# Quarter-array attention scores gathered into one burst per batch, with their exponentials in a ring of their own

## The chip, the cores and the metric

The kernel runs on one core of one Trainium2 chip. The metric is the device time of one execution in microseconds (us); the value used is the median over several runs. A profile of one execution gives the busy times and the chain of waits; its span is 2.1 us shorter than the measured time of the same execution (581.1 against 582.92 us in the run that was profiled, 583.22 us in the median).

## What is computed

```python
def _attn_ref(q, k, v, tau):                     # 8 batches, 12 heads, 448 rows, head size 64
    q_n = q / (np.linalg.norm(q, axis=-1, keepdims=True) + 1e-06)
    k_n = k / (np.linalg.norm(k, axis=-1, keepdims=True) + 1e-06)
    scores = np.matmul(q_n, k_n.transpose(0, 1, 3, 2)) / tau
    attn = np.exp(scores - np.max(scores, axis=-1, keepdims=True))
    attn = attn / (np.sum(attn, axis=-1, keepdims=True) + 1e-09)
    return np.matmul(attn, v)

def _moe_ref(x, U, V, w_ch1, w_ch2):             # x: 8 x 448 x 768, the heads side by side
    h = x.transpose(0, 2, 1) @ U @ V             # low-rank mixing of the rows
    u = x + h.transpose(0, 2, 1)
    return u + np.maximum(u @ w_ch1, 0.0) @ w_ch2    # 768 -> 3072 -> 768
```

The change touches the scores, their exponentials and the product with v, in batches 2 to 7.

## The kernel before, in words

Every operation is first recorded as an `Op` with an engine, an assumed duration, the operations that it depends on, and the ring slots that it acquires and releases. `Plan.run` (L156) then simulates the engines with these assumed durations and fixes the order of the instructions on each engine; the hardware executes each engine's queue in that order. On TensorE there are several streams, each in its own order, and the planner takes the first stream whose head is ready: products with v (`pe_av`) stand ahead of scores (`pe_sc`), and scores ahead of the mixer (`pe_mlp`), so that attention of a later batch is woven into the mixer of an earlier one. `PE`'s order is thus a single line of matmuls, in which the mixer fills all the room.

The stages of a batch b:

- Loads and normalisation: q and k are loaded on the POOL queue (`load_qk`, L493), scaled on VectorE into `xn` (L618), and from batch 2 on transposed by a DMA from the SP queue (L633) into `qkT`. The ring `r_qkT` (L334) has six buffers, one per head pair of a batch; a buffer comes free when the score bursts that read it are issued.
- Scores (`scores`, L661): the 448 keys of a head are cut into three chunks of 128 and a rest of 64. A slot `(p, c)` with c of 0 to 2 is a row slot: two matmuls of 64 rows by 128 columns of the array, one per head of pair p, side by side in the upper and the lower half of the array. A slot `(p, 3)` with p even is a quarter slot: four matmuls of 64 rows by 64 columns, the rest keys of the four heads of pairs p and p+1, one in each quarter of the array (`parts`, L656). All matmuls stream 448 columns. Each slot fills two PSUM banks (`r_sc`, L381, banks 0 to 5), so a burst of three slots takes six banks and is one `Op` on TensorE, planned at 0.2 us and 0.189 us per slot (L680). `groups_of` (L1052) cuts the 21 slots of a batch into seven bursts of three. `mlp` (L994 to L999) ties the bursts to positions in the second product of the mixer two batches earlier (`SPOTS`).
- Exponentials: one ScalarE activation per slot (L695), from PSUM into `attn`. The ring `r_attn` (L326, L329) has three tiles of four chunks; the rest chunk of an even pair also serves the odd pair, so the tile of an even pair is held until the odd pair's products are done (uses 4 against 2, L671).
- Values (`values`, L700): per head 16 matmuls (4 row tiles by 4 key chunks, L718) into one PSUM bank of `r_av2` (L383), then a reciprocal and a multiplication on VectorE (L746, L748) into `X`.
- Mixing (`stage0`, L789): a projection (L801), a product (L851), additions into `u` (L865), a DMA transpose into `uT` (L886). The first burst of a batch also waits for the last products of L851 of the batch before (`first_v`, L1070).
- The mixer (`mlp`, L907): the first product with w_ch1 (L928), a ReLU on ScalarE or VectorE (L951, L953), the second product with w_ch2 (L964), additions (L975), stores (L989).

The bursts of a batch before the change, with pairs written as p.c, are 0.0 0.1 0.2 | 1.0 1.1 1.2 | 0.3 2.0 2.1 | 2.2 3.0 3.1 | 3.2 2.3 4.0 | 4.1 4.2 5.0 | 5.1 5.2 4.3.

Of the kernel before, what the change touches and what calls it, by code (L numbers as in the profile page):

```python
# [269 lines left out]
def kernel(  # L270
# [14 lines left out]
    B, H, S, D = q.shape  # L285
# [3 lines left out]
    NPAIR = H // 2  # L289
# [3 lines left out]
    SC = 4  # L293
    SCH = S // SC
# [5 lines left out]
    BURST = [1] + [2] + [3] * 6  # L300
    SPOTS = {8: [(6,)] * 7 + [()], 6: [(5, 17), (10,), (6,), (6,), (6,), (6,)]}
    WIDE = 2
    RAW_KEYS = {(0, 0), (0, 1)}
    FILL = 0.7

# [6 lines left out]
    def fixed(n, shape, dt, name):  # L312

        tiles = [const.tile(shape, dt, name=f"{name}{i}") for i in range(n)]
        return tiles
# [5 lines left out]
    def fixed_ring(tiles):  # L321
        return Ring(len(tiles), lambda i: tiles[i % len(tiles)])

    ld_t = fixed(3, [SCH, 2, G, SC * D], BF, "qk_nat")
    xn_t = fixed(3, [SCH, 2 * SC, 128], BF, "xn")
    attn_t = fixed(3, [128, SC, 2, 512], BF, "attn")  # L326
    v_t = fixed(2, [128, H, SC, D + 8], BF, "v_nat")

    r_ld, r_xn, r_attn = fixed_ring(ld_t), fixed_ring(xn_t), fixed_ring(attn_t)  # L329
    r_sq = ring(2, [SCH, G // 2, SC * D], BF, "sq")  # L330
    r_ss = ring(4, [SCH, 2, G, SC], FP, "ss")
    r_ln = ring(4, [SCH, 2, G, SC], FP, "ln")
# [29 lines left out]
    r_rd = ring(2, [128, 4, 1], FP, "rd")  # L362
# [3 lines left out]
    def bank_ring(groups, cap, shape=None):  # L366
        def make(g):
            if len(g) > 1:
                return bank_t[:, g[0]:g[-1] + 1, :]
            t_ = bank_t[:, g[0], :]  # L370
            if shape is not None:
                t_ = t_[:, 0:shape[0] * shape[1]].rearrange("p (a b) -> p a b", a=shape[0])
            return t_
        return BankRing(banks, groups, cap, make)

    r_mm = bank_ring([(7,), (6,), (5,), (4,)], 3)
    r_av = bank_ring([(5,), (6,), (7,), (4,)], 2, (4, D + 8))
    r_av0 = bank_ring([(5,), (6,)], 2, (4, D + 8))
    r_av5 = bank_ring([(5,), (6,), (0,), (1,), (2,), (3,)], 2, (4, D + 8))
    r_z = bank_ring([(7,), (4,), (6,), (5,), (3,), (1,), (2,), (0,)], 4)  # L380
    r_sc = bank_ring([(0, 1), (2, 3), (4, 5)], 3)  # L381
    r_low = bank_ring([(5,), (4,), (3,), (2,), (1,), (0,)], 2)
    r_av2 = bank_ring([(5,), (4,), (3,), (2,), (1,), (0,), (6,)], 2, (4, D + 8))  # L383
    r_up = bank_ring([(7,), (6,), (5,), (4,), (3,), (2,), (1,), (0,)], 4)
    r_out = bank_ring([(7,), (6,), (5,), (4,)], 4)
# [23 lines left out]
    plan = Plan()  # L409
# [14 lines left out]
    def pe_t(n):  # L424
        return n / 2400.0 + 0.0025
# [222 lines left out]
        return list(ops.values())  # L648


    attns, bursts = {}, {}

    def members(b, slots):
        return sorted({p for p, _ in slots} | {p + 1 for p, c in slots if b >= WIDE and c == SC - 1})
# [6 lines left out]
    def scores(b, slots, then=()):  # L661

        off = PAD * (b % 2)
        scs = [Slot(r_sc, 2 if (b, p) in RAW_KEYS else 1) for p, _ in slots]
        sets = {p: got[b, p, "qkT"] for p in members(b, slots)}
        ready = []
        for x in sets.values():
            ready += x[1]
        ready += then
        for p in sets:  # L670
            attns.setdefault((b, p), (Slot(r_attn, 2 if b < WIDE or p % 2 else 4), []))  # L671

        def score():
            for (p, c), sc in zip(slots, scs):
                for hh, q_, n0, w, out in parts(b, p, c, sc):
                    qkT, r = sets[q_][0], slice(D * hh, D * hh + D)
                    nc.tensor.matmul(out=out, lhsT=qkT.tile.rearrange("p b s -> p (b s)")[r, n0:n0 + w],  # L677
                                     rhs=qkT.tile[r, SC:2 * SC, :].rearrange("p c s -> p (c s)"),
                                     start=True, stop=True)
        o = plan.add(Op("PE", 0.2 + pe_t(S) * len(slots), score, deps=ready, acq=scs + [attns[b, p][0] for p in sets],  # L680
                        rel=[x[0] for x in sets.values()]), pe_first if b == 0 else pe_sc)
        o.big = len(slots) > 2
        if o.big:
            bursts.setdefault(b, []).append(o)
        for (p, c), sc in zip(slots, scs):
            _, _, (inv, a, scaled) = sets[p]
            attn, exps = attns[b, p]
            if (b, p) in RAW_KEYS:
                for hh in range(2):
                    exps.append(plan.add(Op("ACT", act_t(S, 0.143), lambda sc=sc, c=c, hh=hh, attn=attn, inv=inv, a=a: nc.scalar.activation(  # L690
                        out=attn.tile[0:SCH, c, hh, off:off + S], in_=sc.tile[0:SCH, hh, 0:S], func=AF.Exp,
                        scale=inv.tile[:, 1, a + hh, c:c + 1]), deps=[o, scaled], acq=[attn],
                        rel=[sc, inv], prio=0.1)))
                continue
            exps.append(plan.add(Op("ACT", act_t(2 * S, 0.08), lambda sc=sc, c=c, attn=attn: nc.scalar.activation(  # L695
                out=attn.tile[0:SCH if b < WIDE else 128, c, :, off:off + S],
                in_=sc.tile[0:SCH if b < WIDE else 128, :, 0:S], func=AF.Exp),
                deps=[o], acq=[attn], rel=[sc], prio=0.1 if b == 0 else 1)))

    def values(b, p, X):  # L700
        off = PAD * (b % 2)
        attn, exps = attns[b, p]
        even, kp = attn, SCH
        if b >= WIDE:
            kp = 128
            if p % 2:
                even = attns[b, p - 1][0]
                exps = exps + attns[b, p - 1][1]
        last_exp[b] = exps[-1]
        if b == 0 and p == 0:  # L710
            last_exp["first"] = [exps[0]]
        muls = []
        heads = []
        for hh in range(2):
            heads.append((Slot(r_av2 if BURST[b] > 2 else r_av if b else r_av5 if p == NPAIR - 1 else r_av0, 1), Slot(r_rd, 1)))

        def product(h, hh, t, j, av, start):
            nc.tensor.matmul(out=av.tile[:, t, 0:D + 1],  # L718
                             lhsT=(attn if j < SC - 1 else even).tile[0:kp, j, hh, 128 * t:128 * (t + 1)],
                             rhs=v_t[b % 2][0:kp, h, j, 0:D + 1], start=start, stop=(j == SC - 1),  # L720
                             skip_group_check=ends)
        ends = b == 0 and p == NPAIR - 1
        ready = attn_set + v_set[b]
        if ends:
            for j in range(SC):
                for hh, (av, rd) in enumerate(list(heads)):
                    h = 2 * p + hh

                    def fn(h=h, hh=hh, j=j, av=av):
                        for t in range(4):  # L730
                            product(h, hh, t, j, av, j == 0 and t == 0)
                    o = plan.add(Op("PE", 4 * 0.033, fn, deps=[exps[j]] + got[b, h, "v"] + ready,
                                    acq=[av] if j == 0 else [], rel=[attn] if j == SC - 1 else []), pe_av)
                    if j == SC - 1:
                        heads[hh] += (o,)
        for hh in range(2):
            h = 2 * p + hh
            av, rd = heads[hh][:2]
            o = heads[hh][-1]
            for t in () if ends else range(4):  # L740
                for j in range(SC):
                    first, last = t == 0 and j == 0, t == 3 and j == SC - 1
                    o = plan.add(Op("PE", 0.033, lambda t=t, j=j, h=h, hh=hh, av=av: product(h, hh, t, j, av, j == 0),
                        deps=exps + got[b, h, "v"] + ready if first else (), acq=[av] if first else [],
                        rel=([attn] if even is attn else [attn, even]) if last else []), pe_av)
            r = plan.add(Op("DVE", 0.20, lambda av=av, rd=rd: nc.vector.reciprocal(  # L746
                out=rd.tile, in_=av.tile[:, :, D:D + 1]), deps=[o], acq=[rd], prio=1))
            muls.append(plan.add(Op("DVE", dve_t(256), lambda av=av, rd=rd, h=h: nc.vector.tensor_mul(  # L748
                X.tile[:, :, h * D:(h + 1) * D], av.tile[:, :, 0:D],
                rd.tile.to_broadcast([128, 4, D])), deps=[r],  # L750
                acq=[X], rel=[av, rd], prio=1)))
        last_av[b, p] = o
        return muls
# [298 lines left out]
    def groups_of(b):  # L1052
        if b < WIDE:
            slots = [(p, c) for p in range(NPAIR) for c in range(SC)]
            return [slots[n:n + BURST[b]] for n in range(0, len(slots), BURST[b])]
        slots = []
        for p in range(0, NPAIR, 2):
            slots += [(p, 0), (p, 1), (p, 2), (p + 1, 0), (p + 1, 1), (p + 1, 2), (p, 3)]
        return [slots[n:n + BURST[b]] for n in range(0, len(slots), BURST[b])]

    def go(b, h0, h1, vs=True):
        return stats(b, h0, h1, *load_qk(b, h0, h1), hold=after if b == 1 else ())
# [123 lines left out]
```

## Time and profile before

| | |
|---|---|
| time, median of 3 runs (lowest, highest) | 583.22 us (582.8, 583.4) |
| span of the profiled execution | 581.1 us |
| instructions of TensorE, matmuls | 4871 |
| DVE (VectorE) busy | 292.5 us, 50% |
| ACT (ScalarE) busy | 284.9 us, 49% |
| exponentials L695, 128 x 896 | 166, mean 916 ns |
| granted TensorE clock | full over the whole span |

Durations of single matmuls in the profile overlap[...]. What a matmul costs is read from the start of one to the start of the next, and so from the starts in the timeline; "busy" counts the union of the rows. The timeline merges neighbouring instructions of one line into one row with their number.

### The profile page before, as it was taken

Reading aid. Unit: us, or ns where it says so; the run is one execution under the profiler, and the core shown is the slowest. Engines: PE = TensorE matmul, PEld = TensorE weight load, DVE = VectorE, ACT = ScalarE, POOL = GpSimd, SP = SyncE. Lnnn points to the kernel's source line nnn. Section 1 sums busy time; section 2 is a strip of 40 time slices with the busy share of each in tenths; the row PEclk is TensorE's granted clock in tenths of the full one; section 3 lists DMA queues with packets and bytes.
Section 4 is the critical chain, followed back from the end, with each engine's and each line's share of the span. In section 5 each row is a group of like instructions: output and inputs, shape, how many; then the busy total and the mean of one; then the engine's idle time right before and its main releaser. Section 6 shows DMA issues by size and latency. Waiting matters only on the chain.

```text
span 581.1 us, 11713 instructions
## 1 busy us (share of the span) xinstructions
PE 572.8 (99%) x4871; PEld 327.3 (56%) x4871; DVE 292.5 (50%) x690; ACT 284.9 (49%) x471; POOL 92.9 (16%) x134
## 2 busy tenths in 40 slices
PE   8899999999999999999999999999999999999997
PEld 6565556445655665554466655655456666654565
DVE  8989829999756676557434760343102240100011
ACT  7967754777625671466543645434454334024300
POOL 7334240161050132003300140000000000000000
PEclk9999999999999999999999999999999999999999
DMA  9999992999594469346945573231040100310021
GB/s 156 200 207 191 210 162 69 147 119 116 91 128 107 65 80 145 73 78 79 81 99 91 105 49 68 61 74 33 0 69 28 42 15 11 86 41 1 1 54 56
DMA packets 133429, 50.69 MB, mean 87 GB/s; under 512 B 98304, under 2 KB 133376, under 8 KB 133376
## 3 DMA queue, kind: packets, MB, share of 16 engines
q0 software_dynamic: 72256, 25.73, 39.0%
q1 hardware_dynamic: 61056, 24.19, 20.3%
q8 instruction: 38, 0.62, 0.5%
q14 instruction: 15, 0.12, 0.1%
q10 hardware_dynamic: 64, 0.02, 0.0%
HBM read 52.25 MB, written 11.01 MB: 109 GB/s over the span
## 4 chain that ended last, share of the span: by engine, by line
PE 94%; DMA 2%; DVE 2%; POOL 1%; issue 0%; ACT 0%; DVEq 0%; POOLq 0%
PE bank L964 38%; PE bank L928 37%; PE bank L718 8%; PE bank L677 7%; DMA v_nat<-in_v_dram 2%; PE bank L851 2%; PE bank L474 1%; POOL qk_nat L496 1%; PE bank L801 1%; POOL v_nat L516 0%; DVE xn L618 0%; DVE qkT L1005 0%; PE bank L772 0%; DVE ss L550 0%; DVE X_sb L748 0%
## 5 line engine op out<-in xcount | busy, mean ns | idle before, releaser
L964 PE MATMUL bank<-w_sb,relu 128*128 128x384 bf16 (+1 forms) x1368 | 231.6, 323 | 0.3 <-DVE X_sb L748 0.2
L928 PE MATMUL bank<-uT,w_sb 128*128 128x512 bf16 (+1 forms) x1152 | 231.8, 353 | 0.0
L695 ACT ACTIVATE attn<-bank 128x896 bf16<-128x896 f32 (+1 forms) x166 | 141.0, 916 | 97.8 <-PE bank L677 97.6
L964 PEld LDWEIGHTS <-relu 128*128 128x128 bf16 x1368 | 128.6, 98 | 90.2 <-issue 12.5
L928 PEld LDWEIGHTS <-w_sb 128*128 128x128 bf16 x1152 | 109.1, 98 | 102.3 <-issue 7.6
L951 ACT ACTIVATE relu<-bank 128x384 bf16<-128x384 f32 (+1 forms) x156 | 84.6, 543 | 129.6 <-PE bank L928 129.2
L975 DVE TENSOR_TENSOR O_sb<-bank,u_nat 128x384 f32<-128x384 f32 (+1 forms) x57 | 31.2, 549 | 183.3 <-PE bank L964 165.1
L550 DVE TENSOR_REDUCE ss<-sq 112x8 f32<-112x512 bf16 x96 | 62.5, 674 | 1.6 <-ACT sq L544 1.2
L618 DVE TENSOR_TENSOR xn<-qk_nat,inv 112x512 bf16<-112x512 bf16 x93 | 60.6, 681 | 0.6 <-DMA qkT<-xn 0.5
L718 PEld LDWEIGHTS <-attn 128*128 128x128 bf16 (+1 forms) x1536 | 54.2, 97 | 10.7 <-issue 3.4
L718 PE MATMUL bank<-v_nat,attn 128*128 128x65 bf16 (+1 forms) x1536 | 57.4, 193 | 0.7 <-DMA v_nat<-in_v_dram 0.6
L677 PE MATMUL bank<-qkT 64*128 64x448 bf16 (+1 forms) x384 | 50.2, 358 | 1.3 <-ACT attn L690 0.7
L746 DVE RECIPROCAL rd<-bank 128x4 f32<-128x4 f32 x96 | 16.8, 177 | 58.2 <-PE bank L718 55.5
L496 POOL DMA_DIRECT2D qk_nat<-in_q_dram x24 | 17.5, 727 | 173.2 <-issue 62.7
L748 DVE TENSOR_TENSOR X_sb<-bank,rd 128x256 bf16<-128x256 f32 x96 | 40.2, 421 | 2.0
L544 ACT ACTIVATE sq<-qk_nat 112x512 bf16<-112x512 bf16 x51 | 31.2, 629 | 8.9 <-DVE ss L550 8.5
L519 POOL DMA_DIRECT2D v_nat<-in_v_dram x36 | 26.5, 743 | 48.9 <-PE bank L718 43.4
L953 DVE TENSOR_SCALAR relu<-bank 128x512 bf16<-128x512 f32 (+1 forms) x36 | 22.6, 627 | 14.3 <-PE bank L928 14.1
L677 PEld LDWEIGHTS <-qkT 64*128 64x128 bf16 (+1 forms) x384 | 13.5, 95 | 28.2 <-issue 23.3
L865 DVE TENSOR_TENSOR u_nat<-bank,X_sb 128x384 bf16<-128x384 f32 (+2 forms) x45 | 21.8, 525 | 12.2 <-PE bank L851 12.0
L496 POOL DMA_DIRECT2D qk_nat<-in_k_dram x24 | 16.8, 701 | 5.7 <-DMA w_sb<-in_moe_w_ch_dram 4.3
L546 DVE TENSOR_TENSOR sq<-qk_nat 112x512 bf16<-112x512 bf16 x43 | 16.9, 415 | 0.9 <-DMA qk_nat<-in_q_dram 0.7
(59 smaller groups left out, 187.2 us busy)
## 6 DMA issues: line engine op xcount, KB each, us to landing
qk_nat<-in_q_dram POOLq DMA_DIRECT2D x23, 224.0 KB, 5.4
qk_nat<-in_k_dram POOLq DMA_DIRECT2D x23, 224.0 KB, 6.4
w_sb<-in_moe_w_ch_dram POOLq DMA_DIRECT2D x4, 1152.0 KB, 20.8
w_sb<-in_moe_w_ch_dram POOLq DMA_DIRECT2D x8, 576.0 KB, 16.2
out_dram<-O_sb SPq DMA_DIRECT2D x15, 168.0 KB, 2.3
v_nat<-in_v_dram POOLq DMA_DIRECT2D x14, 168.0 KB, 9.8
out_dram<-O_sb SPq DMA_DIRECT2D x16, 144.0 KB, 2.0
out_dram<-O_sb SPq DMA_DIRECT2D x16, 120.0 KB, 2.2
```

Of the source, the lines that this page charges most:

```text
L496: ops = [load(lambda i=i, src=src: nc.gpsimd.dma_start(out=ld.tile[:, i, lo:lo + h1 - h0, :], in_=src[b, h0:h1].rearrange("h (s c) d -> s ...
L544: nc.scalar.activation(out=y, in_=x, func=AF.Square)
L550: lambda i=i, a0=a0, a1=a1, sq=sq: nc.vector.reduce_sum(ss.tile[:, i, a0:a1, :].rearrange("p h c -> p (h c)"), sq.tile[:, 0:a1 - a0, :].re ...
L618: nc.vector.tensor_mul(dst, src, sc)
L677: nc.tensor.matmul(out=out, lhsT=qkT.tile.rearrange("p b s -> p (b s)")[r, n0:n0 + w], rhs=qkT.tile[r, SC:2 * SC, :].rearrange("p c s -> p ...
L695: exps.append(plan.add(Op("ACT", act_t(2 * S, 0.08), lambda sc=sc, c=c, attn=attn: nc.scalar.activation(out=attn.tile[0:SCH if b < WIDE el ...
L718: nc.tensor.matmul(out=av.tile[:, t, 0:D + 1], lhsT=(attn if j < SC - 1 else even).tile[0:kp, j, hh, 128 * t:128 * (t + 1)], rhs=v_t[b % 2 ...
L748: muls.append(plan.add(Op("DVE", dve_t(256), lambda av=av, rd=rd, h=h: nc.vector.tensor_mul(X.tile[:, :, h * D:(h + 1) * D], av.tile[:, :, ...
L928: o = plan.add(Op("PE", pe_t(n), lambda cc=cc: nc.tensor.matmul(out=mm.tile[:, 0:n], lhsT=w1_sb[:, cc, f * 128:(f + 1) * 128], rhs=uT.tile ...
L951: nc.scalar.activation(out=relu.tile[:, f, 0:n], in_=mm.tile[:, 0:n], func=AF.Relu)
L964: nc.tensor.matmul(out=mm.tile[:, 0:c1 - c0], lhsT=relu.tile[:, f, i * 128:(i + 1) * 128], rhs=w2_t[:, f, c0:c1], start=(f == 0), stop=(f ...
L975: nc.vector.tensor_add(out=O.tile[:, 0:w], in0=mm.tile[:, 0:w], in1=us[i].tile[:, c0:c1]),
```

## The change

From batch 3 on, the three quarter slots of a batch become its first burst, and each of the six bursts that follow holds the three row slots of one pair. The exponentials of the quarter slots go into a ring `r_tail` of their own. It has no memory of its own: its three tiles are chunk 3 of the three `attn` tiles, which the row slots of these batches don't use. An `attn` tile is then held by the two heads of its own pair alone (uses 2), a tail by the four heads of its two pairs. In batch 2 the order of bursts stays, but within a burst the quarter slot is put last.

The first burst now reads all six `qkT` of the batch and acquires three tails. The products of a head use the tail for the last key chunk. From batch 3 on their PSUM banks come from `r_av3`, which lacks bank 6. Two of the planner's assumed durations change: 0.12 us is added per change of kind within a burst, and a product with v of batches 2 to 7 is planned at 0.0305 us in place of 0.033. The aim is fewer changes of array mode within the bursts and earlier release of `attn` tiles.

```diff
+    TB = 3
...
+    tail_t = [t_[:, SC - 1] for t_ in attn_t]
...
+    r_av3 = bank_ring([(5,), (4,), (3,), (2,), (1,), (0,)], 2, (4, D + 8))
     r_av2 = bank_ring([(5,), (4,), (3,), (2,), (1,), (0,), (6,)], 2, (4, D + 8))
...
-        for p in sets:
-            attns.setdefault((b, p), (Slot(r_attn, 2 if b < WIDE or p % 2 else 4), []))
+        into = []
+        for p, c in slots:
+            of, r, n = (tails, r_tail, 4) if b >= TB and c == SC - 1 else (attns, r_attn, 2 if b < WIDE or p % 2 or b >= TB else 4)
+            into.append(of.setdefault((b, p), (Slot(r, n), [])))
...
-        o = plan.add(Op("PE", 0.2 + pe_t(S) * len(slots), score, deps=ready, acq=scs + [attns[b, p][0] for p in sets],
+        kinds = [b >= WIDE and c == SC - 1 for _, c in slots]
+        o = plan.add(Op("PE", 0.2 + pe_t(S) * len(slots) + 0.12 * sum(x != y for x, y in zip(kinds, kinds[1:])), score, deps=ready, acq=scs + [x[0] for n, x in enumerate(into) if x not in into[:n]],
...
-                out=attn.tile[0:SCH if b < WIDE else 128, c, :, off:off + S],
+                out=attn.tile[:, :, off:off + S] if b >= TB and c == SC - 1 else
+                attn.tile[0:SCH if b < WIDE else 128, c, :, off:off + S],
...
-            if p % 2:
+            if b >= TB:
+                tail, more = tails[b, p - p % 2]
+                exps = exps + more
+            elif p % 2:
...
-            heads.append((Slot(r_av2 if BURST[b] > 2 else r_av if b else r_av5 if p == NPAIR - 1 else r_av0, 1), Slot(r_rd, 1)))
+            heads.append((Slot(r_av3 if b >= 3 else r_av2 if BURST[b] > 2 else r_av if b else r_av5 if p == NPAIR - 1 else r_av0, 1), Slot(r_rd, 1)))
...
-                             lhsT=(attn if j < SC - 1 else even).tile[0:kp, j, hh, 128 * t:128 * (t + 1)],
+                             lhsT=tail.tile[:, hh, 128 * t:128 * (t + 1)] if tail and j == SC - 1 else
+                             (attn if j < SC - 1 else even).tile[0:kp, j, hh, 128 * t:128 * (t + 1)],
...
-                    o = plan.add(Op("PE", 0.033, lambda t=t, j=j, h=h, hh=hh, av=av: product(h, hh, t, j, av, j == 0),
+                    o = plan.add(Op("PE", 0.033 if b < 2 else 0.0305, lambda t=t, j=j, h=h, hh=hh, av=av: product(h, hh, t, j, av, j == 0),
...
-                        rel=([attn] if even is attn else [attn, even]) if last else []), pe_av)
+                        rel=([attn, tail] if tail else [attn] if even is attn else [attn, even]) if last else []), pe_av)
...
-        slots = []
-        for p in range(0, NPAIR, 2):
-            slots += [(p, 0), (p, 1), (p, 2), (p + 1, 0), (p + 1, 1), (p + 1, 2), (p, 3)]
-        return [slots[n:n + BURST[b]] for n in range(0, len(slots), BURST[b])]
+        slots = [(p, SC - 1) for p in range(0, NPAIR, 2)] if b >= TB else []
+        for p in range(NPAIR):
+            slots += [(p, c) for c in range(SC - 1)] + ([(p - 1, SC - 1)] if p % 2 and b < TB else [])
+        return [sorted(slots[n:n + BURST[b]], key=lambda x: x[1] == SC - 1) for n in range(0, len(slots), BURST[b])]
```

More of the change, by code (lines that the diff above doesn't have):

```diff
@@ L326 @@
     attn_t = fixed(3, [128, SC, 2, 512], BF, "attn")
+    tail_t = [t_[:, SC - 1] for t_ in attn_t]
     v_t = fixed(2, [128, H, SC, D + 8], BF, "v_nat")
-    r_ld, r_xn, r_attn = fixed_ring(ld_t), fixed_ring(xn_t), fixed_ring(attn_t)
+    r_ld, r_xn, r_attn, r_tail = fixed_ring(ld_t), fixed_ring(xn_t), fixed_ring(attn_t), fixed_ring(tail_t)
     r_sq = ring(2, [SCH, G // 2, SC * D], BF, "sq")
@@ L648, in norm @@
         return list(ops.values())
-    attns, bursts = {}, {}
+    attns, tails, bursts = {}, {}, {}
     def members(b, slots):
@@ L684, in scores @@
             bursts.setdefault(b, []).append(o)
-        for (p, c), sc in zip(slots, scs):
+        for (p, c), sc, (attn, exps) in zip(slots, scs, into):
             _, _, (inv, a, scaled) = sets[p]
-            attn, exps = attns[b, p]
             if (b, p) in RAW_KEYS:
@@ L702, in values @@
         attn, exps = attns[b, p]
-        even, kp = attn, SCH
+        even, kp, tail = attn, SCH, None
         if b >= WIDE:
             kp = 128
-            if p % 2:
+            if b >= TB:
+                tail, more = tails[b, p - p % 2]
+                exps = exps + more
+            elif p % 2:
                 even = attns[b, p - 1][0]
```

## The prediction

> **What bounds the kernel now.** I read the page's first part (busy time by engine), then its chain of waits, then the groups by line, then the waits of TensorE alone, and last the timeline of TensorE over one batch's bursts. From the page:
>
> ```profile
> PE 572.8 (99%) x4871; PEld 327.3 (56%) x4871; DVE 292.5 (50%) x690; ACT 284.9 (49%) x471; POOL 92.9 (16%) x134
> ...
> PE 94%; DMA 2%; DVE 2%; POOL 1%; issue 0%; ACT 0%; DVEq 0%; POOLq 0%
> PE bank L964 38%; PE bank L928 37%; PE bank L718 8%; PE bank L677 7%; DMA v_nat<-in_v_dram 2%; PE bank L851 2%; PE bank L474 1%; POOL qk_nat L496 1%; PE bank L801 1%; POOL v_nat L516 0%; DVE xn L618 0%; DVE qkT L1005 0%; PE bank L772 0%; DVE ss L550 0%; DVE X_sb L748 0%
> ```
>
> TensorE is busy 99% of the span and is 94% of the chain that ended last. The other engines are half busy. So the time is the length of TensorE's single line of matmuls plus the little that it waits. All its waits are in the waits view of TensorE; the lines that concern scores and mixer:
>
> ```profile
> PE bank L677 <- ACT attn L690: 0.7, 3, 0.4
> PE bank L677 <- ACT qkT L1003: 0.4, 1, 0.4
> PE bank L677 <- ACT attn L695: 0.2, 1, 0.2
> PE bank L964 <- DVE X_sb L748: 0.2, 1, 0.2
> ```
>
> These are tenths of a us. The same view from 100 us to the end, which holds all the bursts of batches 2 to 7, has no line at all. A saving can therefore come only from the matmuls themselves, and any wait would be new. The timeline of TensorE around five bursts of batch 4 (start, length of the merged row, matmuls):
>
> ```profile
> 236.29 0.81 PE L964 MATMUL bank<-w_sb,relu 128*128 128x384 bf16 x4
> 237.03 0.87 PE L677 MATMUL bank<-qkT 64*64 64x448 bf16 x8
> 237.83 2.29 PE L964 MATMUL bank<-w_sb,relu 128*128 128x384 bf16 x13
> 239.96 1.14 PE L718 MATMUL bank<-v_nat,attn 128*128 128x65 bf16 x32
> 240.93 1.63 PE L964 MATMUL bank<-w_sb,relu 128*128 128x384 bf16 x9
> 242.39 1.14 PE L718 MATMUL bank<-v_nat,attn 128*128 128x65 bf16 x32
> 243.37 2.11 PE L964 MATMUL bank<-w_sb,relu 128*128 128x384 bf16 x12
> 245.41 0.74 PE L677 MATMUL bank<-qkT 64*128 64x448 bf16 x6
> 246.09 1.64 PE L964 MATMUL bank<-w_sb,relu 128*128 128x384 bf16 x9
> ...
> 250.03 0.97 PE L677 MATMUL bank<-qkT 64*128 64x448 bf16 x8
> 250.93 3.19 PE L928 MATMUL bank<-uT,w_sb 128*128 128x512 bf16 x14
> ...
> 259.46 0.74 PE L677 MATMUL bank<-qkT 64*128 64x448 bf16 x6
> 260.13 3.84 PE L928 MATMUL bank<-uT,w_sb 128*128 128x512 bf16 x17
> 263.91 0.87 PE L677 MATMUL bank<-qkT 64*128 64x448 bf16 x8
> 264.71 1.04 PE L928 MATMUL bank<-uT,w_sb 128*128 128x512 bf16 x4
> ```
>
> From the start of a burst to the start of the next row: the bursts of row slots alone (x6) take 0.68 and 0.67 us; those with a quarter slot first or last (x8) 0.80 and 0.80; that with the quarter slot in the middle 0.90. In all of batches 2 to 7 these three values repeat: 0.674, 0.80 and 0.905 us. So each change of kind inside a burst costs 0.11 to 0.125 us. Entering a burst costs too: 12 matmuls from 243.37 to 245.41 take 2.04, 0.09 more than 12 x 0.1625. A block of 32 value products takes 0.97 (239.96 to 240.93), 30 ns each, with nothing lost at its ends.
>
> [...] within a run of row slots the next slot starts 0.19 to 0.20 us after the one before [...], across a change of kind 0.29 to 0.31. [...] in row bursts the second slot's two loads stand only 11 ns behind the first's. [...] the loads of quarter slots read 103 ns against 93. Two quarter slots in a row occur nowhere in the trace, so how they follow each other is the one unknown price.
>
> **The change, part by part.**
>
> Inner changes of kind, batches 3 to 7. Before, a batch is 4 x 0.674 + 0.80 + 0.905 + 0.80 = 5.20 us of bursts. After, six row bursts are 6 x 0.674 = 4.04. The quarter burst: if the loads of the next quarter slot hide as those of row slots do, it is a row burst, plus 0.024 because the matmul after a quarter slot starts 0.306 after its last one against 0.282, plus 3 x 2 more starts of 3 ns: 0.674 + 0.024 + 0.02, about 0.71 us. [...] it is three times the 0.316 that one takes today before a change, 0.95. [...] I take 0.71, since the four loads of a quarter slot are issued 3 ns apart, as the two of a row slot are. That gives 4.76 per batch, 0.44 saved, 2.2 over five batches.
>
> Batch 2: the quarter slot moves from the middle to the end in one burst, 0.905 to 0.80: 0.1 saved.
>
> Entries: still seven bursts per batch, each entered from a mixer matmul: nothing.
>
> Order of everything else: by the order of the built program TensorE has the same 4871 matmuls in the same numbers per kind (1368 of L964, 1152 of L928, 1536 value products, 312 row and 72 quarter scores, 142 warm-ups). Only the weave changes: more value blocks are split into 16. Since entering or leaving a value block costs nothing (start to start 0.162 before, 0.03 after, in every case), this is free. ScalarE and VectorE have the same exponentials and multiplications; five ReLUs move from VectorE to ScalarE (161 there in place of 156) and one copy of A and three squares change sides, both engines being half idle.
>
> The added waits. The first burst of a batch now needs all six `qkT`, and behind it on TensorE stands the whole mixer. In the trace the last two transposes go out after the last burst, at 264.81, take 2.56 to issue and 3.1 to land: 270.5, while the next batch's first burst starts at 287.98. With the start-to-start times above, the new order puts 20 to 35 us between the last burst of a batch and the first of the next (19 to 32 before), so at least 14 us stay. The tails of the batch before come free with its last value product, which the first burst waited for already through L1070. The products of a pair need the quarter exponential, one burst and more old: hidden. `attn` tiles come free earlier, not later. `r_av3` lacks bank 6, so two of the banks 0 to 5 must come back before the next burst: the shortest stretch from the end of a value block to a burst is 2.04 us (1.72 before), and VectorE needs 0.18 + 0.42 for the last head. The shortest distance of two bursts is 4.50 us (4.23 before) against 2.54 for three exponentials; from the last value block to the projection 2.04 in both. Waits: nothing.
>
> The planner's durations: 0.0305 is closer to the 30 ns seen. The planned burst of quarter slots, 0.77, is within 0.05 of entry plus 0.71. So the order should fit the chip as well as before.
>
> Sum: 2.2 + 0.1 = 2.3 us; 583.22 - 2.3 = 580.9.
>
> **The rivals.** (a) [...] 0.95 per burst, per batch 5.00, saving 0.2 x 5 + 0.1 = 1.1: 582.1. [...] (b) The saving goes into short waits on banks 0 to 5, shared by value products without bank 6 and by bursts: 35 bursts at 0.07 us give 2.3, time 583.2. Against: the distances above all grow or stay. (c) Slower: the first burst catches a late last transpose, since the SP queue now mixes transposes singly with stores; 1 us in each of five batches gives 580.9 + 5 = 585.9. For it: TensorE's queue is strict and everything waits. Against: 14 us of room.
>
> **How the numbers follow.** Forecast 0.78, (a) 0.10, (b) 0.06, (c) 0.06. Predicted 580.9. The runs before spread by 0.4 below the median, so 580.4 is the low end; the high end takes in (a) and 0.3 of spread, 582.4. Faster by over 0.2% means under 582.05: the forecast and most of (a), 0.87. Within 0.2%: the rest of (a) and (b), 0.07. Slower: 0.06.
>
> **What would show it.** In the timeline after: first bursts as x12 rows of 64*64, followed 0.71 later by the mixer (0.95 for (a)); all other bursts of batches 3 to 7 x6 at 0.67; no line in TensorE's waits after 100 us (lines L677 on L695, on the transposes or on L748 for (b) and (c)); the last mixer stretch starting about 2.3 us earlier. The prediction is wrong if such waits appear, or if entering an all-quarter burst costs more than the 0.1 us of any other.

## The result and the profile after

The changed kernel takes 580.37 us (median of 6 runs, 579.89 to 580.82) against 583.03 us for the kernel before (6 runs, 582.78 to 583.94): ratio 0.9953, 95% interval 0.994 to 0.9965, so 2.0 to 3.5 us faster. The forecast was 580.9 with a range from 580.4 to 582.4. The direction and the mechanism hold; the time lies 0.03 us under the range. (The span of a profile is 1.8 us shorter than the time of the same execution, here 578.7 against 580.46 us, and before 581.1 against 582.92; the 2.1 us given further up is the distance to the median.)

The page after, busy time by engine and the chain of waits (line numbers are 5 to 10 higher than before: L682 is the scores, L727 the value products, L938 and L974 the mixer):

```profile
PE 568.3 (98%) x4849; PEld 326.4 (56%) x4871; DVE 287.8 (50%) x683; ACT 288.9 (50%) x478; POOL 93.0 (16%) x134
...
PE 94%; DVE 3%; ACT 1%; issue 1%; DMA 1%; DVEq 0%
PE bank L974 38%; PE bank L938 38%; PE bank L727 8%; PE bank L682 6%; PE bank L861 2%; DVE xn L621 1%; PE bank L477 1%; DVE ss L553 1%; PE bank L811 1%; ACT attn L695 1%; DMA raw_uv<-in_q_dram 1%; DVE qkT L1015 0%; ACT sq L547 0%; PE bank L782 0%; DVE X_sb L758 0%
```

The picture is the same: TensorE is the chain, and only the share of the scores has gone down. (22 of the 4871 matmul records are missing in this trace; a start-to-start time that is one matmul too long comes from that.) The groups by line and shape, row slots and quarter slots, before and after (columns: number, then busy us and mean ns of one):

```profile
L677 PE MATMUL bank<-qkT 64*128 64x448 bf16 x312 | 44.9, 354 | 1.3 <-ACT attn L690 0.7 <-ACT qkT L1003 0.4 <-ACT attn L695 0.2
L677 PE MATMUL bank<-qkT 64*64 64x448 bf16 x72 | 6.9, 373 | 0.0
```
```profile
L682 PE MATMUL bank<-qkT 64*128 64x448 bf16 x312 | 43.0, 353 | 1.2 <-ACT attn L695 0.6 <-ACT qkT L1013 0.5
L682 PE MATMUL bank<-qkT 64*64 64x448 bf16 x72 | 5.0, 360 | 0.0
```

Both kinds of slot are busy for 1.9 us less. Rows that overlap are counted once here, so this shows only that the scores got shorter; what a burst costs is read from the starts.

The timeline of TensorE after, over the bursts of batch 4 (start, length of the merged row, matmuls):

```profile
229.31 0.76 PE L682 MATMUL bank<-qkT 64*64 64x448 bf16 x12
230.01 3.91 PE L974 MATMUL bank<-w_sb,relu 128*128 128x384 bf16 x23
233.85 0.74 PE L682 MATMUL bank<-qkT 64*128 64x448 bf16 x6
234.52 3.91 PE L974 MATMUL bank<-w_sb,relu 128*128 128x384 bf16 x23
238.37 0.74 PE L682 MATMUL bank<-qkT 64*128 64x448 bf16 x6
239.04 3.91 PE L974 MATMUL bank<-w_sb,relu 128*128 128x384 bf16 x23
```

The burst of three quarter slots takes 0.70 us from its start to the next row, the row bursts 0.67. By the start times of the single matmuls it is 0.694 in each of the five batches: the second slot starts 0.203 us after the last matmul of the first, the third 0.179 after that of the second, and the mixer 0.282 after the last. In a row burst the same three distances are 0.196, 0.186 and 0.282. (The matmuls of one slot start 3 to 4 ns apart.) The burst is entered at the price of any other: it starts 0.256 us after the mixer matmul before it, a row burst 0.258. Two narrow windows on the same burst show the third slot with the mixer matmul behind it, and all twelve weight loads, which are over 0.33 us after the burst began, while the third slot starts at 0.40:

```profile
229.72 0.36 PE L682 MATMUL bank<-qkT 64*64 64x448 bf16 x4
230.01 0.34 PE L974 MATMUL bank<-w_sb,relu 128*128 128x384 bf16 x1
```
```profile
229.31 0.33 PEld L682 LDWEIGHTS <-qkT 64*64 64x64 bf16 x12 [0.32 <-issue]
```

So the four loads of a quarter slot, at 102 to 107 ns each, hide as the two of a row slot do, at 92 to 96: the two distances from slot to slot, 0.203 and 0.179 us, sum to the same 0.382 as the 0.196 and 0.186 of a row burst. And TensorE waits nowhere for another engine's result after 100 us; the whole answer of its waits from there on is

```profile
PE bank L938 <- issue: 0.3, 2, 0.2
```

Both stand where a matmul record is missing (behind the burst at 249 us and at 275 us).

Sum of the bursts of batches 2 to 7, by these prices: before 6 x 5.20 = 31.2 us; after 5 x (6 x 0.674 + 0.694) + 5.09 = 28.8 us, where 5.09 is batch 2, whose three mixed bursts now take 0.798 each. The difference is 2.4 us. The stretch from the first burst of batch 2 to the end of the span went from 581.1 - 108.4 = 472.7 to 578.7 - 108.5 = 470.2 us, 2.5 less. That is the whole effect, as long as no new wait eats it; the experiments on bank 6 below show how one can.

### The profile page after: what moved, and what is told of

Read it like the earlier page. It is cut to its first block, busy times and chain, and to the rows that moved or that the text cites. A ratio compares the mean times of both kernels' runs of the same rounds, so it can differ in the third digit from the quotient of the medians.

```text
span 578.7 us, 11692 instructions
## 1 busy us (share of the span) xinstructions
PE 568.3 (98%) x4849; PEld 326.4 (56%) x4871; DVE 287.8 (50%) x683; ACT 288.9 (50%) x478; POOL 93.0 (16%) x134
## 4 chain that ended last, share of the span: by engine, by line
PE 94%; DVE 3%; ACT 1%; issue 1%; DMA 1%; DVEq 0%
PE bank L974 38%; PE bank L938 38%; PE bank L727 8%; PE bank L682 6%; PE bank L861 2%; DVE xn L621 1%; PE bank L477 1%; DVE ss L553 1%; PE bank L811 1%; ACT attn L695 1%; DMA raw_uv<-in_q_dram 1%; DVE qkT L1015 0%; ACT sq L547 0%; PE bank L782 0%; DVE X_sb L758 0%
## 5 line engine op out<-in xcount | busy, mean ns | idle before, releaser
L974 PE MATMUL bank<-w_sb,relu 128*128 128x384 bf16 (+1 forms) x1368 | 232.0, 323 | 0.3 <-DVE X_sb L758 0.2
L938 PE MATMUL bank<-uT,w_sb 128*128 128x384 bf16 (+1 forms) x1131 | 229.9, 352 | 1.3 <-issue 0.3
L974 PEld LDWEIGHTS <-relu 128*128 128x128 bf16 x1368 | 128.4, 98 | 91.9 <-issue 14.2
L938 PEld LDWEIGHTS <-w_sb 128*128 128x128 bf16 x1152 | 108.7, 98 | 101.0 <-issue 7.2
L961 ACT ACTIVATE relu<-bank 128x384 bf16<-128x384 f32 (+1 forms) x161 | 87.6, 545 | 133.5 <-PE bank L938 132.1
L985 DVE TENSOR_TENSOR O_sb<-bank,u_nat 128x384 f32<-128x384 f32 (+1 forms) x57 | 31.2, 549 | 189.5 <-PE bank L974 165.6
L727 PEld LDWEIGHTS <-attn 128*128 128x128 bf16 (+1 forms) x1536 | 54.9, 97 | 11.2 <-issue 2.8
L727 PE MATMUL bank<-v_nat,attn 128*128 128x65 bf16 (+1 forms) x1536 | 58.1, 193 | 0.2
L682 PE MATMUL bank<-qkT 64*128 64x448 bf16 (+1 forms) x384 | 47.7, 354 | 1.2 <-ACT attn L695 0.6
L547 ACT ACTIVATE sq<-qk_nat 112x512 bf16<-112x512 bf16 x54 | 32.8, 632 | 9.7 <-DVE ss L553 9.4
L682 PEld LDWEIGHTS <-qkT 64*128 64x128 bf16 (+1 forms) x384 | 13.0, 96 | 24.5 <-issue 19.0
L963 DVE TENSOR_SCALAR relu<-bank 128x384 bf16<-128x384 f32 (+1 forms) x31 | 19.2, 618 | 14.8 <-PE bank L938 14.6
```

The lines of the kernel that those rows point to most:

```text
L547: nc.scalar.activation(out=y, in_=x, func=AF.Square)
L727: nc.tensor.matmul(out=av.tile[:, t, 0:D + 1], lhsT=tail.tile[:, hh, 128 * t:128 * (t + 1)] if tail and j == SC - 1 else (attn if j < SC - ...
L938: o = plan.add(Op("PE", pe_t(n), lambda cc=cc: nc.tensor.matmul(out=mm.tile[:, 0:n], lhsT=w1_sb[:, cc, f * 128:(f + 1) * 128], rhs=uT.tile ...
L961: nc.scalar.activation(out=relu.tile[:, f, 0:n], in_=mm.tile[:, 0:n], func=AF.Relu)
L974: nc.tensor.matmul(out=mm.tile[:, 0:c1 - c0], lhsT=relu.tile[:, f, i * 128:(i + 1) * 128], rhs=w2_t[:, f, c0:c1], start=(f == 0), stop=(f ...
L985: nc.vector.tensor_add(out=O.tile[:, 0:w], in0=mm.tile[:, 0:w], in1=us[i].tile[:, c0:c1]),
```

## The experiments

Theory 1: the time is the length of TensorE's line, and only the inner changes of kind (from row slots to a quarter slot or back; the forecasts say array mode) were taken out of it. Theory 2: the rings, the banks and the planner's durations give a better order, and the saving is theirs. All ratios are to the kernel before, run on the same chip.

**Rings without the new bursts, and more changes of kind.** e1 keeps everything of the change but the order of slots:

```diff
-        slots = [(p, SC - 1) for p in range(0, NPAIR, 2)] if b >= TB else []
-        for p in range(NPAIR):
-            slots += [(p, c) for c in range(SC - 1)] + ([(p - 1, SC - 1)] if p % 2 and b < TB else [])
-        return [sorted(slots[n:n + BURST[b]], key=lambda x: x[1] == SC - 1) for n in range(0, len(slots), BURST[b])]
+        slots = []
+        for p in range(0, NPAIR, 2):
+            slots += [(p, 0), (p, 1), (p, 2), (p + 1, 0), (p + 1, 1), (p + 1, 2), (p, 3)]
+        return [slots[n:n + BURST[b]] for n in range(0, len(slots), BURST[b])]
```

> The changed kernel with its rings, banks and planner durations, but with the bursts of the kernel before (quarter slots spread, four inner changes of kind per batch). Theory 1, the saving is the inner changes of array mode: bursts of 0.80, 0.905 and 0.80 us return, 5.20 us per batch, and the time is that of the kernel before, 583.0 us (ratio 1.000). Theory 2, the saving is the earlier release of attn tiles and a better order: it stays at 580.4 us (ratio 0.9955).

e3 then puts each quarter slot in the middle of its burst:

```diff
-        return [slots[n:n + BURST[b]] for n in range(0, len(slots), BURST[b])]
+        cut = [sorted(slots[n:n + BURST[b]], key=lambda x: x[1] == SC - 1) for n in range(0, len(slots), BURST[b])]
+        return [[x[0], x[2], x[1]] if x[2][1] == SC - 1 else x for x in cut]
```

> As e1, but each of the three mixed bursts of a batch has its quarter slot in the middle, so six inner changes per batch in place of four, in batches 2 to 7. Theory 1: 4 x 0.674 + 3 x 0.905 = 5.41 us of bursts per batch, 0.21 more than before, 1.27 over six batches: 584.3 us (ratio 1.002). Theory 2, inner changes don't matter since other work fills in: 580.4 to 583.0 us.

e4 has no quarter bursts and no tails; the quarter slot is last in its burst in all six batches:

```diff
-    TB = 3
+    TB = 8
```

> The changed kernel without quarter bursts and tails; within the bursts of all six batches the quarter slot is put last. Three inner changes per batch: 4 x 0.674 + 3 x 0.798 = 5.09 us of bursts, 0.11 less than before, 0.65 over six batches. Theory 1 (inner changes alone): ratio 0.9989, a quarter of the whole saving for none of the rings. Rival, an order with waits of its own: at or above 1.000, with waits of TensorE after 100 us.

Measured, with the sum of bursts by their prices (0.674; 0.80 or 0.798 with the quarter slot first or last; 0.905; 0.694), and the stretch from the first burst of batch 2 to the end of the span. The stretch is of the one profiled execution, the time is the median of all:

| kernel | inner changes, all batches | bursts, us | stretch, us | time, us | ratio (95% interval) |
|---|---|---|---|---|---|
| e3_middle | 36 | 32.5 | 474.2 | 584.19 | 1.0024 (1.0016 to 1.0033) |
| before | 24 | 31.2 | 472.7 | | 1 |
| e1_rings_only | 24 | 31.2 | 472.9 | 583.18 | 1.0009 (1.0002 to 1.0015) |
| e4_sort_only | 18 | 30.5 | 472.1 | 582.48 | 0.9997 (0.9989 to 1.0005) |
| changed kernel | 3 | 28.8 | 470.2 | 580.37 | 0.9953 (0.994 to 0.9965) |

The stretch less the bursts is 441.4 to 441.8 in all five. Between the ends of the table, 36 inner changes and 3, each is worth 0.12 us of the stretch, and the ratios give about the same. The rings alone bring nothing: e1 is even 0.5 us slower in the median, more than its bursts explain. Theory 2 falls in this form. The medians follow less closely than the stretches: for e4 0.65 us less was expected, its stretch gives 0.6, its ratio only 0.2, with an interval that holds 1 and, at its end, the forecast 0.9989. Why the medians of e1 and e4 lie higher than their stretches is open. In e3 the mixed bursts are, in the timeline of TensorE, all of the long kind:

```profile
239.99 0.97 PE L682 MATMUL bank<-qkT 64*128 64x448 bf16 x8
246.85 0.74 PE L682 MATMUL bank<-qkT 64*128 64x448 bf16 x6
252.86 0.97 PE L682 MATMUL bank<-qkT 64*128 64x448 bf16 x8
```

**The planner's durations and bank 6.** e2 undoes three small lines of the change and keeps its bursts:

```diff
-+ 0.12 * sum(x != y for x, y in zip(kinds, kinds[1:]))
-0.033 if b < 2 else 0.0305
+0.033
-r_av3 if b >= 3 else r_av2
+r_av2
```

> The changed kernel with the planner's durations of before (0.033 per value product, no 0.12 per change of kind) and with bank 6 allowed for value products. Theory 1: the bursts stay as in the changed kernel (0.694 for the quarter burst, 0.674 for the others) and TensorE doesn't wait, so 580.4 us (ratio 0.9955). Theory 2, part of the saving comes from an order that fits the chip better: some of 2.4 us is lost, 581 to 582.5 us, with waits of TensorE after 100 us.

Measured: 584.36 us, ratio 1.0024 (1.0014 to 1.0034). That is 4 us more than the changed kernel, and slower than the kernel before. Neither theory had a loss of this size. The bursts are as forecast, the waits are not. So e6 undoes the bank alone, and e7 the duration of a value product alone (the 0.12 us per change of kind was not undone alone):

> The changed kernel with one line undone: value products of batches 3 to 7 may take bank 6 again. e2 lost 4.2 us in waits of TensorE on banks (its mixer on L758 and L985), with bank 6 and the old durations together. Theory A, bank 6 did it, because the mixer's second product takes banks 7 and 6 first: most of e2's 4 us return, ratio to before about 1.002, with waits of L974 on L758 and L985 after 100 us. Theory B, the durations did it: ratio 0.9955, no waits after 100 us.

> The changed kernel with one number undone: a value product is planned at 0.033 us again, where the chip takes 0.030, so each block of 32 is planned 0.09 us late. Theory A (bank 6): ratio 0.9955, no waits after 100 us. Theory B (durations): ratio about 1.002 with TensorE waiting on banks after value blocks.

Measured: e6 583.76 us, ratio 1.0022 (1.0012 to 1.0031); e7 580.01 us, ratio 0.9955 (0.9942 to 0.9967). The duration of a value product does not matter; bank 6 carries nearly the whole of e2. The stretch from the first burst of batch 2 is 473.6 us in e6 against 470.2. (The profiled execution of e6, at 585.74 us, lost another 2 us ahead of that stretch: its first burst of batch 2 starts at 584.0 - 473.6 = 110.4 us, against 108.5. The cause is open.) The waits of TensorE in e6 after 100 us:

```profile
PE bank L938 <- DVE relu L963: 1.3, 2, 0.7
PE bank L974 <- DVE O_sb L985: 0.8, 2, 0.7
PE bank L974 <- DVE X_sb L758: 0.4, 1, 0.4
PE bank L727 <- issue: 0.2, 1, 0.2
PE bank L938 <- issue: 0.2, 1, 0.2
```

One of them in the timeline, first TensorE, then VectorE:

```profile
194.25 0.65 PE L727 MATMUL bank<-v_nat,attn 128*128 128x65 bf16 x16
194.73 0.33 PE L938 MATMUL bank<-uT,w_sb 128*128 128x384 bf16 x1
195.71 0.48 PE L938 MATMUL bank<-uT,w_sb 128*128 128x384 bf16 x2 [0.65 <-DVE relu L963]
```
```profile
194.93 0.18 DVE L756 RECIPROCAL rd<-bank 128x4 f32<-128x4 f32 x1 [1.55 <-PE bank L727]
195.10 0.56 DVE L963 TENSOR_SCALAR relu<-bank 128x384 bf16<-128x384 f32 x1
195.57 0.41 DVE L758 TENSOR_TENSOR X_sb<-bank,rd 128x256 bf16<-128x256 f32 x1
```

A value block of one head (x16) ends; one mixer matmul follows, and the next has to wait until VectorE has emptied a bank by the ReLU L963. VectorE's reciprocal, ahead of the ReLU in its queue, waited 1.55 us for that value block; the ReLU starts at 195.10, 0.37 us after the last mixer matmul ahead of the wait, and ends at 195.66, and the next mixer matmul starts at 195.71. Such a pattern costs 0.98 - 0.16 = 0.82 us from start to start, three times in e6; four more places lose 0.16 to 0.57 each, 3.8 us in all.

Why bank 6? The planner's own record of which PSUM bank each operation gets says it: in the kernel before and in the changed kernel the mixer's products are given bank 6 or 7 in all but about 15 of 249 cases, mostly in turn, and no value block of batches 2 to 7 gets either. In e6 21 of the 60 heads of batches 3 to 7 get bank 6, in e2 22 (e1, e4 and e7 withhold it, as the changed kernel does). In the kernel before, bank 6 was open to value blocks too, as the last choice, but its order never needed it: with it withheld there, the planner's order comes out the same. In the new order it is taken often.

It is taken in places that would otherwise stay free of value blocks: in e6 11 of the 21 heads are planned less than 2 us behind a burst and the other ten less than 1.5 us ahead of the next, where banks 0 to 5 belong to the burst; in the changed kernel no value block from 150 us on is planned nearer than 2.88 us behind one, and in its trace none ends nearer than 2.04 us ahead of one. While such a block sits in bank 6, the mixer mostly has bank 7 alone: at the wait shown above the planner gave the value block bank 6, and the mixer product that waits got bank 7, the bank that the mixer had left one matmul before and that the ReLU had still to empty.

To test this against mere chance of the order, e13 opens bank 7 in place of 6:

```diff
-    r_av3 = bank_ring([(5,), (4,), (3,), (2,), (1,), (0,)], 2, (4, D + 8))
+    r_av3 = bank_ring([(5,), (4,), (3,), (2,), (1,), (0,), (7,)], 2, (4, D + 8))
```

> The changed kernel in which the value products of batches 3 to 7 may take bank 7, as the last choice, in place of bank 6; the planner gives it to 19 of their 60 heads (bank 6 in e6: 21 of 60; in the changed kernel and in the kernel before neither bank is ever given to them). Theory A, the mixer works in banks 6 and 7 in turn and a value block in either leaves it one bank: as e6, ratio to before about 1.002, with waits of TensorE on L963, L985 or L758 after 100 us. Rival, something particular to bank 6 or mere chance of the order: ratio 0.9955, without such waits.

Measured: 582.61 us, ratio 0.9997 (0.9988 to 1.0005), and the waits of TensorE after 100 us are

```profile
PE bank L974 <- DVE X_sb L758: 1.0, 1, 1.0
PE bank L938 <- DVE X_sb L758: 0.2, 1, 0.2
PE bank L974 <- DVE O_sb L985: 0.2, 1, 0.2
```

2.5 us of the changed kernel's gain are lost, not 4 as theory A had it: its direction and its kind of wait are there, the size is smaller. In the longest of these waits the mixer product was planned into bank 7 itself, one matmul behind a value block there. Why 19 heads on bank 7 cost less than 21 on bank 6 is open.

**The quarter burst in batch 2 too.** e5 extends the change by one batch:

```diff
-    TB = 3
+    TB = 2
```

> The changed kernel with the quarter burst in batch 2 as well. Theory 1: the bursts of batch 2 fall from 4 x 0.674 + 3 x 0.798 = 5.09 to 6 x 0.674 + 0.694 = 4.74, 0.35 us less: 580.0 us (ratio 0.9949). Rival: in batch 2 the six transposed pairs and the three tails come straight after batch 1, whose exponentials still use chunk 3 of the attn tiles; the first burst or the mixer behind it waits, and the time is 580.4 us or more, with a wait of TensorE between 95 and 130 us.

Measured: 581.92 us, ratio 0.998 (0.9974 to 0.9987), slower than the changed kernel by 1.6 us. The quarter burst of batch 2 starts at 127.2 instead of the first row burst at 108.5: in the planner's record it is the last of the six transposes that it starts behind, and the order of everything after it changes. TensorE then loses 0.8 us at 183 and 0.5 at 150, start to start, both on VectorE, and not between 95 and 130 us as the rival had it:

```profile
PE bank L938 <- DVE sq L549: 0.7, 1, 0.7
PE bank L974 <- DVE X_sb L758: 0.4, 1, 0.4
```

In e5 three value heads of batch 2 have bank 6. So e9 withholds bank 6 from batch 2 as well, and e10 is the same kernel run for its trace:

```diff
-r_av3 if b >= 3 else r_av2
+r_av3 if b >= 2 else r_av2
```

> e5 (quarter burst in batch 2 too) with bank 6 withheld from the value products of batch 2 as well. e5 waited about 1.5 us: 0.5 at 150, 0.7 at 183 and 0.3 us at 188. Theory A (bank 6 in batch 2 did it): these waits go, and the 0.35 us of batch 2 is gained on top of the changed kernel, ratio about 0.995. Rival (the order after batch 2 is off by itself, for example a ReLU behind squares on VectorE): waits of a few tenths stay, ratio 0.997 to 0.999.

> The same kernel as e9, for a trace. e9 was slow by 0.5% although no value block is on banks 6 or 7. In its order the first burst of batch 3 is followed at once by a row burst, with no mixer matmul between. Theory: the mixer has nothing ready there, so TensorE waits for the three quarter exponentials of 2.5 us to free the banks; about 2 to 3 us of wait at one place near 180 us, on L700. Rival: many waits of tenths, as in e6.

Measured: e9 586.04 us, ratio 1.0054 (1.0042 to 1.0066); e10 585.88 us, ratio 1.0052 (two runs). Both forecasts of e9, 0.995 and 0.997 to 0.999, were wrong. The timeline of TensorE in e10:

```profile
180.69 0.76 PE L682 MATMUL bank<-qkT 64*64 64x448 bf16 x12
182.10 0.36 PE L682 MATMUL bank<-qkT 64*128 64x448 bf16 x2 [0.64 <-ACT attn L700]
182.90 0.36 PE L682 MATMUL bank<-qkT 64*128 64x448 bf16 x2 [0.44 <-ACT attn L700]
183.71 0.36 PE L682 MATMUL bank<-qkT 64*128 64x448 bf16 x2 [0.45 <-ACT attn L700]
186.49 3.79 PE L938 MATMUL bank<-uT,w_sb 128*128 128x384 bf16 x12 [2.41 <-DMA uT<-u_nat]
```

The next mixer product has not got its transposed input, so nothing lies between the two bursts; the row slots wait for the quarter exponentials one by one (1.5 us, less than the 2 to 3 us expected), then the mixer for the DMA (2.4 us, not expected). After that hole the row of twelve mixer matmuls is 3.79 us long, where a row of twelve is 2.11 in the kernel before (at 243.37). The windows of the same trace (us, PE busy, then the granted clock ahead of the DMA share) show the clock there:

```profile
186.50:190.00 3.50, 3.50 (x12) 1.72 (x13) 0.50 (x1) 1.01 (x2) 0.00 (x0) 0.53 0.20 45
190.00:194.00 4.00, 4.00 (x28) 2.00 (x26) 2.67 (x7) 3.34 (x6) 0.00 (x0) 0.99 0.29 57
```

A mean clock of 0.53 over these 3.5 us goes with 1.7 us more for the twelve matmuls. The three parts make 5.6 us, and e10 is 5.7 us above the changed kernel by the ratios. Last, e11 is e5 with the old duration for value products, which gives another order:

> e5 (quarter burst in batch 2 too) with the value product planned at 0.033 us. Its order has 4 value heads of batch 2 on bank 6 and no two bursts side by side. If the bank is what costs: a few waits of 0.3 to 0.8 us against 0.35 us gained in batch 2, ratio 0.996 to 0.998. If it has no waits, it beats the changed kernel: ratio 0.9949.

Measured: 579.86 us, ratio 0.995 (0.9937 to 0.9962). TensorE has a single wait of 0.2 us after 100 us, although four heads of batch 2 have bank 6, one more than in e5. So bank 6 does not explain e5 by itself; which order an extension falls into decides, and what makes e5's order wait at 183 is open. e11 is the fastest median of all, but its interval overlaps that of the changed kernel (0.994 to 0.9965), and the two are not told apart here.

## Why the prediction was right and where it was wrong

The mechanism was right. One term of the sum was mis-sized, and the range left too little room for it.

- "TensorE is the chain, and any wait would be new": right. The stretch less the bursts is the same before and after (441.5 and 441.4 us).
- Inner changes of kind at 0.11 to 0.125 us: right, and shown by five kernels with 3 to 36 of them. (From slot to slot a change of kind reads 0.28 to 0.32 us, not 0.29 to 0.31. The traces show what a change costs, not why.) Batch 2 at 0.1 saved and entries at nothing: right.
- The quarter burst at 0.71: this is the step that failed, by its size. It measures 0.694. (The prediction's own terms, 0.674 + 0.024 + 0.02, give 0.718.) The term "plus 0.024 because the matmul after a quarter slot starts 0.306 after its last one" is wrong: 0.306 was seen only behind a quarter slot that itself follows a matmul of another shape; behind the third of three it is 0.282, as behind a row slot. This makes 0.46 per batch in place of 0.44, 2.4 in place of 2.3 in all. Rival (a), three times the 0.316 that a quarter slot takes before a change, so 0.95, is out.
- The low end of the range, 580.4: too close. It left 0.5 us for the spread of runs and nothing for the baseline (583.03 in place of 583.22 when measured again, 0.2 us) or for a quarter burst cheaper than assumed (0.1 us). The measured 580.37 is 0.03 below, less than the spread of its own runs (579.89 to 580.82), so on which side of 580.4 it fell was chance. By the spans the saving was 2.4 us, by the medians 2.7, and the interval holds both; the 0.3 between them is not explained.
- "Waits: nothing": right in the result. The distances in the order came out as forecast: 2.04 us from a value block to a burst and 4.52 us between bursts at the least, and the last transpose of a batch lands 15.5 us or more before its quarter burst. Rival (b), short waits at the bursts for banks 0 to 5, is not in the trace. (Its 35 times 0.07 us make 2.45, not 2.3; nothing hangs on that.)
- Bank 6: the step that I read from the wrong side. I entered its loss as a cost to be hidden, and rival (b) as waits "shared by value products without bank 6". The runs show that withholding it is what holds the gain: with it, the same bursts are at 1.0022, 3.4 us by the stretch and 4 by the ratios above the changed kernel, and slower than the kernel before. I asked only what the value blocks need, not who else lives in bank 6; the mixer, which is three quarters of the chain, has banks 6 and 7 nearly to itself. That "waits: nothing" came true rests on this line, which the prediction gave no credit: it was right there without knowing why.
- Rival (c), a late first burst because it needs all six transposed pairs: not in batches 3 to 7, where there was room. In batch 2 the same need moves the first burst by nearly 19 us.

## What to carry to other kernels

When one engine's queue is the whole time, price its instructions from start to start by what stands before and after each, and multiply: changes of kind inside a burst were 0.11 to 0.125 us apiece in every variant. A change that makes a queue denser can open a conflict that the old order never reached: for each shared buffer, ask who else is given it while the engine that sets the time is running on it. Where a planner fixes the order, a small edit can give an order that waits for several us (5.7 us in e10), so look at the waits before trusting the sum.

## What the runs showed of the hardware

- Three quarter slots in a row cost 0.694 us, 0.02 more than three row slots at 0.674, although each brings four weight loads in place of two. In the trace after, the four loads of a slot start 3 to 4 ns apart and read 102 to 107 ns each (92 to 96 in row slots), and the last of the twelve ends 0.33 us after the burst began.
- In the trace before, the source lines of all 4871 matmuls, and of 470 instructions of ScalarE and 669 of VectorE, stand in the order of the built program: none was started ahead of its turn.
- In e10 TensorE did only three short pieces of work between 181.4 and 186.5 us (the longest single wait was 2.4 us). Its clock read 1.00 from 183.8 to 186.4, averaged 0.53 from 186.5 to 190, and read 0.99 in the 4 us after that. This is one place in one run.
